# Interleaved partitions for shifted copies, deeper load buffers and a DMA server in the list schedule of an attention and gated convolution kernel

## The chip, the cores and the metric

The kernel runs on one core of a Trainium2 chip. The metric is device time in microseconds (us) of one launch; the kernel before takes 236.15 us, the median of three runs (235.55 to 236.35). The profiled execution has a span of 233.1 us from its first to its last instruction; times inside it are counted from its start.

Names used: PE is TensorE (PEld its weight loads), DVE is VectorE, ACT is ScalarE, POOL is GpSimd, SP is SyncE, whose queue issues nearly all DMAs here. PSUM has eight banks of 128 x 512 floats in this program.

## The reference

Four batches, eight heads, 768 positions, head size 64. Attention is causal, and a query sees only the six chunks of 32 keys with the highest upper bound. The result goes, with heads side by side (512 channels), through a gated unit whose gate is a causal depthwise convolution of five taps.

```python
k_chunks = k.reshape(B, H, nc, chunk, D)                 # chunk = 32, nc = 24
k_min, k_max = np.min(k_chunks, axis=3), np.max(k_chunks, axis=3)
ub = np.sum(np.maximum(q[:, :, :, None, :] * k_min[:, :, None, :, :],
                       q[:, :, :, None, :] * k_max[:, :, None, :, :]), axis=-1)
ub = np.where(causal, ub, -1e9)
top_chunks = np.argsort(ub, axis=-1)[..., -6:]
scores = scale * np.matmul(q, k.transpose(0, 1, 3, 2))
scores = np.where(sel & causal_by_position, scores, -1e9) # sel: the key's chunk is among the six
attn = softmax(scores)
x = np.matmul(attn, v)                                   # then [B, S, 512]

for k in range(5):
    gate_pre += conv_w[k][None, None, :] * xp[:, k:k + S, :]   # xp: x with 4 zero rows ahead
gate = 1.0 / (1.0 + np.exp(-gate_pre))
out = (gate * (x @ w_val)) @ w_out
```

## The kernel before

Work goes by pairs of heads: 16 pairs (0 to 15), four to a batch. For each pair q, k and v are loaded, q and k transposed on PE (`ktr`, `qtr`), the chunk bounds formed (`ub`, `top`), the selection transposed (`selT`), scores computed (`sc`), exponentials taken on ACT (`ex`), multiplied with v (`av`), normalised, and transposed into `xT` (`tox`). The convolution of a pair (`cv`) and, once for each batch of four pairs, the value product (`val`), the gating (`gv`) and the output product (`out`) follow.

Every step is an operation of a graph. A list schedule, run when the program is built, puts the operations of each engine and the DMA issues into a fixed order, and gives each PSUM tile its bank; on the chip each engine works through its own order and waits on semaphores. An operation has an engine, the time that it holds it (`occ`), a latency and a key that ranks it:

```python
NBUF = dict(kn=3, qn=3, vn=3, Kh=3, Qh=3, ql=2, rh=2, rl=2, km=2, KB=2, VA=3, mub=2, top=2, NS=2,
            MT=2, on=2, xT=8, XS=3, g=8, gv=8, osb=3, scr=4)
...
    def op(self, name, eng, occ, key, emit, r=(), w=(), war=(), ps=(), lat=None, mode=None, after=()):
...
                    o.end = t + occ - o.occ + o.lat
```

The loads, two DMAs for each tensor and pair, one for each head:

```python
        def load(name, p=p, b_=b_, h0=h0):
            def emit():
                src = getattr(t, name[0])
                for hh in range(2):
                    t.nc.sync.dma_start(out=vv(name, p)[:, :, hh * 64:(hh + 1) * 64],
                                        in_=src[b_, h0 + hh].rearrange("(t p) d -> p t d", p=128))
            return emit
        for x, name in enumerate(("kn", "qn", "vn")):
            G.op(f"{name}{p}", "SP", 1.1, key("load", p, x + (3 if x == 2 else 0)), load(name), w=[(name, p)], lat=3.2)
```

The convolution uses shifted copies of `xT`. The 128 channels of a pair, in four groups of 32, go to DRAM (`scr`, one row for each of 32 channels, the four groups side by side), and come back four times (`XS`): into partitions 0 to 31 and 32 to 63 as they are, into 64 to 95 and 96 to 127 three positions further on. Blocks 0 and 2 meet the high part of the taps in the matmul, blocks 1 and 3 the low part, so one matmul of 128 rows covers taps o and o + 3 in two precisions. `WD` holds the diagonals of taps that fit this order of partitions.

```python
        def xw(p=p):
            t.nc.sync.dma_start(out=t.scr[p % 4].rearrange("c (g n) -> g c n", g=4), in_=t.xT[:, p % 8, :])

        def xs(p=p):
            n = 4 * XW
            for blk in range(4):
                sh = 3 * (blk // 2)
                t.nc.sync.dma_start(out=vv("XS", p)[32 * blk:32 * blk + 32, 0:n - 3], in_=t.scr[p % 4][:, sh:sh + n - 3])
        G.op(f"xw{p}", "SP", 0.55, key("xs", p), xw, r=[("xT", p)], w=[("scr", p)], lat=2.6)
        G.op(f"xs{p}", "SP", 2.2, key("xs", p, 0.1), xs, r=[("scr", p)], w=[("XS", p)], lat=4.6)

        def conv(w, p=p):
            def emit():
                ...
                for o in range(3):
                    for g in range(4):
                        t.nc.tensor.matmul(out=b[32 * g:32 * g + 32, 0:HB], lhsT=t.WD[:, o * 16 + (p % 4) * 4 + g, :],
                                           rhs=x[:, g * XW + w * HB + o:g * XW + w * HB + o + HB], start=(o == 0), stop=(o == 2))
```

The output tiles: a product into PSUM, an eviction by ACT into one of the `osb` buffers, a store.

```python
        def outev(s, b_=b_):
            def emit():
                t.nc.scalar.activation(out=vv("osb", 6 * b_ + s), in_=bank(("out", b_, s)), func=AF.Copy, scale=0.5)
            return emit

        def outdma(s, b_=b_):
            def emit():
                t.nc.sync.dma_start(out=t.out[b_, s * 128:(s + 1) * 128, :], in_=vv("osb", 6 * b_ + s))
            return emit
```

The weights `wval` and `wout` are loaded once from GpSimd's queue, with a cast to 16 bits.

Of the kernel before, what the change touches and what calls it, by code (L numbers as in the profile page):

```python
# [46 lines left out]
for _bi, _segs in enumerate(BANKS):  # L47
    for _col, _jt, _q0, _n in _segs:
        for _i in range(_n // 128):
            WHERE[_jt, _q0 // 128 + _i] = (_bi, _col + 128 * _i)  # L50

NBUF = dict(kn=3, qn=3, vn=3, Kh=3, Qh=3, ql=2, rh=2, rl=2, km=2, KB=2, VA=3, mub=2, top=2, NS=2,
            MT=2, on=2, xT=8, XS=3, g=8, gv=8, osb=3, scr=4)

PERIOD = 9.537
OFF = dict(load=-38.8, ktr=-26.25, qtr=-23.06, kev=-7.55, qev=-7.41, ksm=-26.91, spl=-1.52, vc=6.87,
# [3 lines left out]

class Op:
    __slots__ = ("name", "eng", "occ", "lat", "emit", "key", "deps", "succ", "ps", "n", "ready", "start",
                 "end", "idx", "mode")


class Graph:
# [3 lines left out]
        self.nbuf, self.ops = nbuf, []  # L70
        self.reads, self.writes, self.wars, self.after = {}, {}, [], []

    def op(self, name, eng, occ, key, emit, r=(), w=(), war=(), ps=(), lat=None, mode=None, after=()):
        o = Op()
        o.name, o.eng, o.occ, o.emit, o.key, o.ps = name, eng, occ, emit, key, tuple(ps)
# [12 lines left out]
        return o  # L88
# [21 lines left out]
    def schedule(self, nbank=8):  # L110
# [8 lines left out]
        mode = None  # L119
        ready = {e: [] for e in ENG}  # L120
        for o in ops:
            o.n, o.ready = len(o.deps), 0.0
# [7 lines left out]
        while events:  # L130
            t = heapq.heappop(events)
            while events and events[0] <= t + 1e-9:
                heapq.heappop(events)
            while releases and releases[0][0] <= t + 1e-9:
                rt, b = heapq.heappop(releases)
                freeb.append((rt, b))
            again = True
            while again:
                again = False
                for e in ENG:  # L140
# [32 lines left out]
                    if e == "PE":  # L173
                        if o.mode != mode:
                            occ += MODE_SWITCH
                        mode = o.mode
                    o.end = t + occ - o.occ + o.lat
                    free_at[e] = t + occ
                    for x in o.ps:
                        b = home[x]  # L180
# [24 lines left out]
ENG = ("PE", "ACT", "DVE", "POOL", "SP")  # L205
SEM = dict(PE=0.24, ACT=0.15, DVE=0.13, POOL=0.10, SP=0.0)
MODE_SWITCH = 0.08


def mm(n, cols):  # L210
# [19 lines left out]
def graph(off, period, nbuf):  # L230
    G = Graph(nbuf)
    t = T()

    def key(stage, p, x=0.0):
        return p * period + off[stage] + x

    def bank(x):
        return t.psb[G.home[x]]
# [4 lines left out]
    def vv(name, v):  # L243
        a = t.tiles[name]
        return a[v % nbuf[name]]
# [58 lines left out]


    def w_cw():
        for b in range(4):
            t.nc.sync.dma_start(out=t.cw4[:, b, :], in_=t.conv_w.rearrange("k (c d) -> (k c) d", d=32))
    kd = 0.9 * period
    G.op("cw", "SP", 2.0, kd + off["load"] + 2 * period, w_cw, w=[("cw4",)], lat=4.0)  # L310
# [4 lines left out]
    G.op("wbig", "POOL", 2.4, 2.2 * period, w_big, w=[("wbig",)], lat=14.0)  # L315

    def w_tr():
        t.nc.tensor.transpose(out=bank("cwT")[:, 0:80], in_=t.cw4.rearrange("p b d -> p (b d)"),
                              identity=t.ident[0:80, 0:80])
    G.op("cwT", "PE", 0.12, 1.2 * period, w_tr, r=[("cw4",), ("ident",)], ps=["cwT"])  # L320

    def w_split():
        nc, b = t.nc, bank("cwT")
        nc.vector.memset(t.wsel, 0.0)
        nc.vector.tensor_copy(out=t.whi, in_=b[:, 0:80])
        nc.vector.tensor_tensor(out=t.wlo, in0=b[:, 0:80], in1=t.whi, op=ALU.subtract)
        for blk in range(4):
            ps_ = slice(32 * blk, 32 * blk + 32)
            src = (t.whi, t.wlo)[blk % 2]
            lo, n = (0, 48) if blk < 2 else (48, 32)  # L330
            nc.vector.tensor_copy(out=t.wsel[ps_, 0:n], in_=src[ps_, lo:lo + n])
            nc.vector.tensor_copy(out=t.id4[ps_, :], in_=t.ident[ps_, ps_])
    G.op("wsplit", "DVE", 1.6, 1.2 * period, w_split, r=[("cwT",), ("ident",)], w=[("wsel",)], ps=["cwT"],
         after=[G.ops[-1]])

    def w_diag(j):
# [9 lines left out]
    for p in range(NPAIR):  # L346
# [3 lines left out]
        def load(name, p=p, b_=b_, h0=h0):  # L350
            def emit():
                src = getattr(t, name[0])
                for hh in range(2):
                    t.nc.sync.dma_start(out=vv(name, p)[:, :, hh * 64:(hh + 1) * 64],  # L354
                                        in_=src[b_, h0 + hh].rearrange("(t p) d -> p t d", p=128))
            return emit
        for x, name in enumerate(("kn", "qn", "vn")):
            G.op(f"{name}{p}", "SP", 1.1, key("load", p, x + (3 if x == 2 else 0)), load(name), w=[(name, p)], lat=3.2)


        def tr(name, w, p=p):
# [74 lines left out]
        G.op(f"rlo{p}", "DVE", dve(640), key("spl", p, 0.1), rlo, r=[("Qh", p), ("ql", p)], w=[("rl", p)])  # L436

        def vcast(p=p):
            t.nc.gpsimd.tensor_copy(out=vv("VA", p)[:, :, :, 0:D].rearrange("p h t d -> p t h d"),
                                    in_=vv("vn", p).rearrange("p t (h d) -> p t h d", h=2))  # L440
        G.op(f"vc{p}", "POOL", 1.05, key("vc", p), vcast, r=[("vn", p), ("ones",)], w=[("VA", p)])


# [147 lines left out]
        def xs(p=p):  # L591
            n = 4 * XW
            for blk in range(4):
                sh = 3 * (blk // 2)
                t.nc.sync.dma_start(out=vv("XS", p)[32 * blk:32 * blk + 32, 0:n - 3], in_=t.scr[p % 4][:, sh:sh + n - 3])
        G.op(f"xw{p}", "SP", 0.55, key("xs", p), xw, r=[("xT", p)], w=[("scr", p)], lat=2.6)
        G.op(f"xs{p}", "SP", 2.2, key("xs", p, 0.1), xs, r=[("scr", p)], w=[("XS", p)], lat=4.6)

        def conv(w, p=p):
            def emit():  # L600
# [20 lines left out]
    for b_ in range(B):  # L621
# [89 lines left out]
def kernel(  # L711
# [17 lines left out]
    def tl(name, shape, dt=FP):  # L729
        return cp.tile(shape, dt, tag=name, name=name)  # L730
# [10 lines left out]
    t.cw4 = tl("cw4", [80, 4, 32])  # L741
    t.whi = tl("whi", [128, 80], F16)
    t.wlo = tl("wlo", [128, 80])
    t.wsel = tl("wsel", [128, 48])
# [8 lines left out]
    shapes = dict(kn=([128, NT, 128], FP), qn=([128, NT, 128], FP), vn=([128, NT, 128], FP), Kh=([128, S], F16),  # L753
                  Qh=([128, S], F16), ql=([128, 640], F16), rh=([128, 640], F16), rl=([128, 640], F16),
                  km=([128, 2, NCH], FP), KB=([128, 2, 2, 2 * NCH], F16), VA=([128, 2, NT, D + 1], F16),
                  mub=([128, NIT, 2 * NCH], FP), top=([128, NIT, 2, 8], FP), NS=([128, NIT, 128], F16),
# [36 lines left out]
```

The softmax here doesn't subtract the row's maximum and nothing guards it: scores larger than these inputs give would overflow.

## Time and profile before

| What | Value |
|---|---|
| time, median of three | 236.15 us |
| span of the profiled execution | 233.1 us |
| PE busy | 191.0 us, 82% |
| DVE busy | 148.2 us, 64% |
| ACT busy | 142.7 us, 61% |
| POOL busy | 96.3 us, 41% |
| DMA by the hardware queue | 41.06 MB, 81.5% of 16 engines |
| mean granted PE clock | 0.912 |

Each view is read as follows. The strip cuts the span into 40 equal slices; a digit is the busy share of a slice in tenths, and for PEclk the granted clock in tenths of full speed. A wait names the engine and line that waited, what released it, the total, how often, and the longest. The chain of waits is followed back from the last instruction; its pieces are given in order of time. A stretch line gives busy time of each engine in the stretch, with the number of instructions, then the clock, the DMA share and the rate. A DMA share above one means that more than one packet at a time was open on an engine.

The DMA issues of the page (KB of one, median us from issue to landing):

```profile
XS<-scr SPq DMA_DIRECT2D x64, 193.3 KB, 4.3
kn<-in_k_dram SPq DMA_DIRECT2D x32, 192.0 KB, 6.3
qn<-in_q_dram SPq DMA_DIRECT2D x32, 192.0 KB, 6.4
vn<-in_v_dram SPq DMA_DIRECT2D x32, 192.0 KB, 5.3
out_dram<-osb SPq DMA_DIRECT2D x24, 256.0 KB, 4.7
scr<-xT SPq DMA_DIRECT2D x16, 193.5 KB
```

### The profile page before, as it was taken

What the parts mean: (1) busy time and instruction counts of PE and PEld (TensorE: products, weight loads), DVE (VectorE), ACT (ScalarE), POOL (GpSimd) and SP (SyncE); (2) the same over time, 40 slices, a digit from 0 to 9 for tenths busy, and PEclk for the clock granted to TensorE, in tenths of its full rate; (3) what the DMA queues carried; (4) which work ended last, traced back from release to release, by engine and by line L of the source; (5) the groups of instructions that cost most, each with busy time, mean ns of one, the idle gap of its engine ahead of it and who ended that gap; (6) DMA issues with size and microseconds to landing.
All of it is one profiled execution on the core that took longest, in us unless ns stands there. A gap on an engine that the chain in (4) does not pass through costs nothing.

```text
span 233.1 us, 7133 instructions
## 1 busy us (share of the span) xinstructions
PE 191.0 (82%) x2713; PEld 129.4 (56%) x2713; DVE 148.2 (64%) x481; ACT 142.7 (61%) x313; POOL 96.3 (41%) x216
## 2 busy tenths in 40 slices
PE   7476599999999994999991059999999999941993
PEld 3364396778666754484750028668475675511441
DVE  2687679999999994688590006998955355300340
ACT  2342849998998893777760055997766982301233
POOL 8766926576874771635260002746422130000000
PEclk9769779999999999799999558999999999995599
DMA  7999999989998999699999999596377845468133
GB/s 158 218 218 140 221 221 209 211 200 187 219 170 200 193 201 185 145 197 178 194 182 196 240 225 212 156 211 167 97 198 192 241 98 145 123 180 257 46 132 138
DMA packets 85377, 42.55 MB, mean 183 GB/s; under 512 B 77152, under 2 KB 80224, under 8 KB 85344
## 3 DMA queue, kind: packets, MB, share of 16 engines
q1 hardware_dynamic: 84288, 41.06, 81.5%
q0 software_dynamic: 1056, 1.05, 2.8%
q8 instruction: 21, 0.34, 0.7%
q14 instruction: 12, 0.10, 0.2%
HBM read 33.68 MB, written 9.46 MB: 185 GB/s over the span
## 4 chain that ended last, share of the span: by engine, by line
PE 45%; DVE 18%; DMA 18%; SPq 10%; issue 4%; ACT 3%; DVEq 0%; ACTq 0%
PE b L628 9%; SPq L354 7%; PE b L605 7%; PE b L652 7%; DMA scr<-xT 5%; DMA qn<-in_q_dram 5%; PE b L365 5%; PE b L554 5%; DMA kn<-in_k_dram 4%; DVE km L377 4%; PE b L510 4%; DVE on L563 4%; PE b L451 3%; PE b L515 3%; DVE ql L415 2%
## 5 line engine op out<-in xcount | busy, mean ns | idle before, releaser
L524 ACT ACTIVATE P<-b 128x512 f16<-128x512 f32 (+1 forms) x192 | 88.3, 584 | 13.6 <-PE b L515 9.6
L532 POOL TENSOR_SCALAR_AFFINE_SELECT P<-P 128x512 f16<-128x512 f16 (+1 forms) x64 | 35.2, 570 | 53.5 <-ACT P L524 52.8
L510 PE MATMUL b<-Qh,Kh 64*128 64x128 f16 (+3 forms) x384 | 40.5, 269 | 13.3 <-ACT osb L658 13.2
L515 PE MATMUL b<-MT,E 64*128 64x128 f16 (+4 forms) x352 | 38.4, 266 | 1.3 <-DVE MT L496 1.3
L377 DVE TENSOR_REDUCE km<-b 128x12 f32<-128x384 f32 x64 | 33.0, 547 | 9.0 <-POOL P L532 3.8
L636 DVE SCALAR_TENSOR_TENSOR gv<-g,b 128x384 f16<-128x384 f32 x32 | 17.5, 549 | 32.0 <-PE b L628 31.4
L658 ACT ACTIVATE osb<-b 128x512 f32<-128x512 f32 x24 | 14.4, 621 | 35.2 <-DMA out_dram<-osb 25.0
L605 PE MATMUL b<-XS,WD 128*32 128x384 f16 x384 | 22.1, 358 | 7.9 <-DMA XS<-scr 7.9
L515 PEld LDWEIGHTS <-E 64*128 64x128 f16 x352 | 18.0, 98 | 18.5 <-issue 15.7
L554 PEld LDWEIGHTS <-P 128*128 128x128 f16 x672 | 24.4, 99 | 4.9 <-issue 2.5
L554 PE MATMUL b<-VA,P 128*128 128x65 f16 x672 | 26.7, 196 | 0.5 <-DVE on L563 0.3
L371 ACT ACTIVATE Kh<-b 128x384 f16<-128x384 f32 x32 | 16.1, 512 | 17.0 <-PE b L365 10.1
L510 PEld LDWEIGHTS <-Kh 64*128 64x128 f16 x384 | 18.8, 97 | 12.4 <-issue 7.9
L628 PE MATMUL b<-xT,wval 128*128 128x384 f16 x128 | 25.6, 344 | 0.0
L652 PE MATMUL b<-wout,gv 128*128 128x512 f16 x96 | 22.2, 380 | 0.1
L407 ACT ACTIVATE Qh<-b 128x384 f16<-128x384 f32 x32 | 14.7, 499 | 11.4 <-PE b L365 11.3
L611 ACT ACTIVATE g<-b 128x384 f32<-128x384 f32 x32 | 15.5, 512 | 9.2 <-PE b L605 4.4
L584 DVE COPY xT<-b 128x768 f16<-128x768 f16 x16 | 8.8, 549 | 19.0 <-PE b L579 16.6
L365 PE MATMUL b<-ident,kn 128*128 128x128 f32 x96 | 15.0, 294 | 6.7 <-DMA kn<-in_k_dram 5.6
L365 PE MATMUL b<-ident,qn 128*128 128x128 f32 x96 | 15.0, 291 | 4.7 <-DMA qn<-in_q_dram 4.7
L563 DVE TENSOR_TENSOR on<-b,rcp 128x384 f16<-128x384 f32 x32 | 17.8, 557 | 1.1
L605 PEld LDWEIGHTS <-WD 128*32 128x32 f16 x384 | 8.9, 101 | 17.1 <-DMA XS<-scr 8.7
(62 smaller groups left out, 322.7 us busy)
## 6 DMA issues: line engine op xcount, KB each, us to landing
XS<-scr SPq DMA_DIRECT2D x64, 193.3 KB, 4.3
kn<-in_k_dram SPq DMA_DIRECT2D x32, 192.0 KB, 6.3
qn<-in_q_dram SPq DMA_DIRECT2D x32, 192.0 KB, 6.4
vn<-in_v_dram SPq DMA_DIRECT2D x32, 192.0 KB, 5.3
out_dram<-osb SPq DMA_DIRECT2D x24, 256.0 KB, 4.7
scr<-xT SPq DMA_DIRECT2D x16, 193.5 KB
wval<-in_moe_w_val_dram POOLq DMA_DIRECT2D x1, 512.0 KB, 7.0
wout<-in_moe_w_out_dram POOLq DMA_DIRECT2D x1, 512.0 KB, 9.9
```

What stands on the lines that cost most here:

```text
L365: t.nc.tensor.transpose(out=b[:, j * 128:(j + 1) * 128], in_=vv(name, p)[:, 3 * w + j, :], identity=t.ident)
L377: t.nc.vector.tensor_reduce(out=vv("km", p)[:, i, w * 12:(w + 1) * 12], in_=bank(("kn", p, w))[:, 0:HB].rearrange("p (c t) -> p c t", t=CH ...
L510: nc.tensor.matmul(out=bb[hh][:, col:col + n], lhsT=kh[HP[hh], jt * 128:(jt + 1) * 128], rhs=qh[HP[hh], q0:q0 + n], start=(si == 0), stop= ...
L515: nc.tensor.matmul(out=bb[hh][:, col + m0 - q0:col + n], lhsT=t.E[HP[hh], jt * 128:(jt + 1) * 128], rhs=mt[HP[hh], m0 - 128:q0 + n - 128], ...
L524: t.nc.scalar.activation(out=t.P[p % 2][hh][bi], in_=bank(("s", p, bi, hh))[:, 0:n], func=AF.Exp, scale=0.125 / QS)
L532: t.nc.gpsimd.affine_select(out=ap, in_=ap, pattern=[[0, n], [1, 128]], compare_op=ALU.is_ge, fill=0.0, base=0, channel_multiplier=-1)
L554: t.nc.tensor.matmul(out=b[:, qt, :], lhsT=t.P[p % 2][hh][bi][:, col:col + 128], rhs=vv("VA", p)[:, hh, jt, :], start=(jt == 0), stop=(jt ...
L563: t.nc.vector.tensor_tensor(out=vv("on", p)[:, :, hh * 64:(hh + 1) * 64], in0=b[:, :, 0:D], in1=rc.unsqueeze(2).to_broadcast([128, NT, D]) ...
L605: t.nc.tensor.matmul(out=b[32 * g:32 * g + 32, 0:HB], lhsT=t.WD[:, o * 16 + (p % 4) * 4 + g, :], rhs=x[:, g * XW + w * HB + o:g * XW + w * ...
L628: t.nc.tensor.matmul(out=k[:, 0:HB], lhsT=t.wval[:, ct, et * 128:(et + 1) * 128], rhs=t.xT[:, (4 * b_ + ct) % 8, 4 + w * HB:4 + (w + 1) * HB],
L636: t.nc.vector.scalar_tensor_tensor(out=vv("gv", 4 * b_ + et)[:, sl], in0=vv("g", 4 * b_ + et)[:, sl], scalar=1.0, in1=bank(("val", b_, et, ...
L652: t.nc.tensor.matmul(out=k, lhsT=vv("gv", 4 * b_ + et)[:, s * 128:(s + 1) * 128], rhs=t.wout[:, et, :], start=(et == 0), stop=(et == NCT - 1))
```

## The change

The four shifted copies are laid out with a partition step of 4: channel d of copy b goes to partition 4d + b, where it was 32b + d. The filter's taps, their high and low parts and the diagonal blocks are prepared for that order (masks made from the identity choose, by partition modulo 4, high or low part and taps o or o + 3). v of a pair comes in one DMA, in an order that the cast to 16 bits reads straight through; the filter comes in one DMA and is replicated by DVE. There are five buffers for q, k and v and four for the output. The list schedule treats DMA as a server that takes one transfer after another, so that it no longer counts on a fixed latency for each; the order of all engines follows from that.

```diff
-NBUF = dict(kn=3, qn=3, vn=3, Kh=3, Qh=3, ql=2, rh=2, rl=2, km=2, KB=2, VA=3, mub=2, top=2, NS=2,
-            MT=2, on=2, xT=8, XS=3, g=8, gv=8, osb=3, scr=4)
+NBUF = dict(kn=5, qn=5, vn=5, Kh=3, Qh=3, ql=2, rh=2, rl=2, km=2, KB=2, VA=3, mub=2, top=2, NS=2,
+            MT=2, on=2, xT=8, XS=3, g=8, gv=8, osb=4, scr=4)
@@ the schedule @@
                     o.end = t + occ - o.occ + o.lat
+                    if o.dma:
+                        dma_free = max(dma_free, t + DMA_HEAD) + o.dma
+                        o.end = max(t + occ, dma_free) + DMA_TAIL
+DMA_HEAD, DMA_TAIL = 1.0, 1.3
@@ the filter @@
-        for b in range(4):
-            t.nc.sync.dma_start(out=t.cw4[:, b, :], in_=t.conv_w.rearrange("k (c d) -> (k c) d", d=32))
+        t.nc.sync.dma_start(out=t.cw, in_=t.conv_w.rearrange("k (c d) -> (k c) d", d=32))
+    def w_rep():
+        t.nc.vector.tensor_copy(out=t.cw4, in_=t.cw.unsqueeze(2).to_broadcast([80, 32, 4]))
-        nc.vector.memset(t.wsel, 0.0)
-        nc.vector.tensor_copy(out=t.whi, in_=b[:, 0:80])
-        nc.vector.tensor_tensor(out=t.wlo, in0=b[:, 0:80], in1=t.whi, op=ALU.subtract)
-        for blk in range(4):
-            ...                       # two copies of 32 partitions for each block
+        v.tensor_reduce(out=t.pm[:, 0:4], in_=t.ident.rearrange("p (c b) -> p b c", b=4), axis=AX.X, op=ALU.add)
+        v.tensor_reduce(out=t.id4, in_=c4, axis=AX.X, op=ALU.add)
+        ...                           # nine more operations on up to 80 columns
@@ the loads @@
+                dst, src = vv(name, p), src[b_, h0:h0 + 2]
+                if name == "vn":
+                    t.nc.sync.dma_start(out=dst, in_=src.rearrange("h (t p) d -> p h t d", p=128))
+                    return
-            G.op(f"{name}{p}", "SP", 1.1, key("load", p, x + (3 if x == 2 else 0)), load(name), w=[(name, p)], lat=3.2)
+            G.op(f"{name}{p}", "SP", 0.6 if x == 2 else 1.1, key("load", p, x + (3 if x == 2 else 0)), load(name), w=[(name, p)], dma=1.8)
@@ the cast of v @@
-            t.nc.gpsimd.tensor_copy(out=vv("VA", p)[:, :, :, 0:D].rearrange("p h t d -> p t h d"),
-                                    in_=vv("vn", p).rearrange("p t (h d) -> p t h d", h=2))
+            t.nc.gpsimd.tensor_copy(out=vv("VA", p)[:, :, :, 0:D], in_=vv("vn", p))
@@ the shifted copies @@
-                t.nc.sync.dma_start(out=vv("XS", p)[32 * blk:32 * blk + 32, 0:n - 3], in_=t.scr[p % 4][:, sh:sh + n - 3])
-        G.op(f"xw{p}", "SP", 0.55, key("xs", p), xw, r=[("xT", p)], w=[("scr", p)], lat=2.6)
-        G.op(f"xs{p}", "SP", 2.2, key("xs", p, 0.1), xs, r=[("scr", p)], w=[("XS", p)], lat=4.6)
+                t.nc.sync.dma_start(out=vv("XS", p)[blk::4, 0:n - 3], in_=t.scr[p % 4][:, sh:sh + n - 3])
+        G.op(f"xw{p}", "SP", 0.55, key("xs", p), xw, r=[("xT", p)], w=[("scr", p)], dma=0.5)
+        G.op(f"xs{p}", "SP", 2.2, key("xs", p, 0.1), xs, r=[("scr", p)], w=[("XS", p)], dma=2.0)
@@ the output stores @@
-            G.op(f"od{b_}.{s}", "SP", 0.6, key("ev", p3, x), outdma(s), r=[("osb", 6 * b_ + s)], lat=2.2)
+            G.op(f"od{b_}.{s}", "SP", 0.6, key("ev", p3, x), outdma(s), r=[("osb", 6 * b_ + s)], dma=0.65)
```

More of the change, by code (lines that the diff above doesn't have):

```diff
@@ L62 @@
     __slots__ = ("name", "eng", "occ", "lat", "emit", "key", "deps", "succ", "ps", "n", "ready", "start",
-                 "end", "idx", "mode")
+                 "end", "idx", "mode", "dma")
 class Graph:
@@ L71, in __init__, with op @@
         self.reads, self.writes, self.wars, self.after = {}, {}, [], []
-    def op(self, name, eng, occ, key, emit, r=(), w=(), war=(), ps=(), lat=None, mode=None, after=()):
+    def op(self, name, eng, occ, key, emit, r=(), w=(), war=(), ps=(), lat=None, mode=None, after=(), dma=None):
         o = Op()
+        o.dma = dma
         o.name, o.eng, o.occ, o.emit, o.key, o.ps = name, eng, occ, emit, key, tuple(ps)
@@ L118, in schedule @@
         free_at = {e: 0.0 for e in ENG}
-        mode = None
+        mode, dma_free = None, 0.0
         ready = {e: [] for e in ENG}
@@ L306, in w_cw @@
     def w_cw():
-        for b in range(4):
-            t.nc.sync.dma_start(out=t.cw4[:, b, :], in_=t.conv_w.rearrange("k (c d) -> (k c) d", d=32))
+        t.nc.sync.dma_start(out=t.cw, in_=t.conv_w.rearrange("k (c d) -> (k c) d", d=32))
     kd = 0.9 * period
-    G.op("cw", "SP", 2.0, kd + off["load"] + 2 * period, w_cw, w=[("cw4",)], lat=4.0)
+    G.op("cw", "SP", 0.6, kd + off["load"] + 2 * period, w_cw, w=[("cw",)], lat=3.0)
     def w_big():
@@ L315, in graph @@
     G.op("wbig", "POOL", 2.4, 2.2 * period, w_big, w=[("wbig",)], lat=14.0)
+    def w_rep():
+        t.nc.vector.tensor_copy(out=t.cw4, in_=t.cw.unsqueeze(2).to_broadcast([80, 32, 4]))
+    G.op("cwrep", "DVE", 0.25, 1.2 * period, w_rep, r=[("cw",)], w=[("cw4",)])
     def w_tr():
-        t.nc.tensor.transpose(out=bank("cwT")[:, 0:80], in_=t.cw4.rearrange("p b d -> p (b d)"),
+        t.nc.tensor.transpose(out=bank("cwT")[:, 0:80], in_=t.cw4.rearrange("p d b -> p (d b)"),
                               identity=t.ident[0:80, 0:80])
@@ L323, in w_split @@
         nc, b = t.nc, bank("cwT")
-        nc.vector.memset(t.wsel, 0.0)
-        nc.vector.tensor_copy(out=t.whi, in_=b[:, 0:80])
-        nc.vector.tensor_tensor(out=t.wlo, in0=b[:, 0:80], in1=t.whi, op=ALU.subtract)
-        for blk in range(4):
[L328 to L333, printed above, removed]
+        v, c4 = nc.vector, t.ident.rearrange("p (c b) -> p c b", b=4)
+        v.tensor_reduce(out=t.pm[:, 0:4], in_=t.ident.rearrange("p (c b) -> p b c", b=4), axis=AX.X, op=ALU.add)
+        v.tensor_reduce(out=t.id4, in_=c4, axis=AX.X, op=ALU.add)
+        v.tensor_tensor(out=t.pm[:, 4:6], in0=t.pm[:, 0:2], in1=t.pm[:, 2:4], op=ALU.add)
+        v.tensor_tensor(out=t.pm[:, 6:7], in0=t.pm[:, 0:1], in1=t.pm[:, 1:2], op=ALU.add)
+        v.tensor_tensor(out=t.pm[:, 7:8], in0=t.pm[:, 2:3], in1=t.pm[:, 3:4], op=ALU.add)
+        v.tensor_copy(out=t.whi, in_=b[:, 0:80])
+        v.tensor_tensor(out=t.wlo, in0=b[:, 0:80], in1=t.whi, op=ALU.subtract)
+        v.tensor_scalar(out=t.wlo, in0=t.wlo, scalar1=t.pm[:, 5:6], scalar2=None, op0=ALU.mult)
+        v.scalar_tensor_tensor(out=t.wlo, in0=t.whi, scalar=t.pm[:, 4:5], in1=t.wlo, op0=ALU.mult, op1=ALU.add)
+        v.tensor_scalar(out=t.wsel, in0=t.wlo[:, 0:48], scalar1=t.pm[:, 6:7], scalar2=None, op0=ALU.mult)
+        v.scalar_tensor_tensor(out=t.wsel[:, 0:32], in0=t.wlo[:, 48:80], scalar=t.pm[:, 7:8], in1=t.wsel[:, 0:32],
+                               op0=ALU.mult, op1=ALU.add)
+    G.op("wsplit", "DVE", 2.0, 1.2 * period, w_split, r=[("cwT",), ("ident",)], w=[("wsel",)], ps=["cwT"],
          after=[G.ops[-1]])
@@ L352, in emit @@
                 src = getattr(t, name[0])
+                dst, src = vv(name, p), src[b_, h0:h0 + 2]
+                if name == "vn":
+                    t.nc.sync.dma_start(out=dst, in_=src.rearrange("h (t p) d -> p h t d", p=128))
+                    return
                 for hh in range(2):
-                    t.nc.sync.dma_start(out=vv(name, p)[:, :, hh * 64:(hh + 1) * 64],
-                                        in_=src[b_, h0 + hh].rearrange("(t p) d -> p t d", p=128))
+                    t.nc.sync.dma_start(out=dst[:, :, hh * 64:(hh + 1) * 64],
+                                        in_=src[hh].rearrange("(t p) d -> p t d", p=128))
             return emit
         for x, name in enumerate(("kn", "qn", "vn")):
-            G.op(f"{name}{p}", "SP", 1.1, key("load", p, x + (3 if x == 2 else 0)), load(name), w=[(name, p)], lat=3.2)
+            G.op(f"{name}{p}", "SP", 0.6 if x == 2 else 1.1, key("load", p, x + (3 if x == 2 else 0)), load(name), w=[(name, p)], dma=1.8)
         def tr(name, w, p=p):
@@ L740 @@
     t.E = tl("E", [128, S], F16)
-    t.cw4 = tl("cw4", [80, 4, 32])
+    t.cw = tl("cw", [80, 32])
+    t.cw4 = tl("cw4", [80, 32, 4])
+    t.pm = tl("pm", [128, 8])
     t.whi = tl("whi", [128, 80], F16)
@@ L752 @@
     t.P = [[[tl(f"P{i}_{hh}{bi}", [128, WIDTH[bi]], F16) for bi in range(6)] for hh in range(2)] for i in range(2)]
-    shapes = dict(kn=([128, NT, 128], FP), qn=([128, NT, 128], FP), vn=([128, NT, 128], FP), Kh=([128, S], F16),
+    shapes = dict(kn=([128, NT, 128], FP), qn=([128, NT, 128], FP), vn=([128, 2, NT, D], FP), Kh=([128, S], F16),
                   Qh=([128, S], F16), ql=([128, 640], F16), rh=([128, 640], F16), rl=([128, 640], F16),
```

## The prediction

> **What bounds the kernel now.** I read the strip of 40 slices first, then the wait list, the queue's own waits, the chain of waits around the two large holes, and last the busy time per stretch. The strip (slices of 5.8 us):
>
> ```profile
> PE   7476599999999994999991059999999999941993
> ...
> PEclk9769779999999999799999558999999999995599
> DMA  7999999989998999699999999596377845468133
> ```
>
> TensorE (PE) is full in most slices and is the bound there. It has three holes: the first six slices, slices 21 to 23 (about 122 to 137 us), and slices 35 to 37 (about 204 to 216 us). The DMA row is full up to slice 24, so transfers are the second bound of the first 140 us. After each of the two later holes the granted clock is 5, half speed. The waits name who holds the middle hole:
>
> ```profile
> engine line waited for: us in total, times, longest us
> ...
> ACT osb L658 <- DMA out_dram<-osb: 25.0, 4, 13.8
> ...
> PE b L510 <- ACT osb L658: 13.2, 1, 13.2
> ```
>
> The score matmul L510 waits 13.2 us in one piece for ScalarE's eviction `osb`, which waits 13.8 us because the tile that was in this buffer before, three output tiles earlier, hasn't gone out. The waits of the queue itself:
>
> ```profile
> SPq L595 <- DMA scr<-xT: 45.1, 12, 5.6
> ```
>
> SyncE's queue is in order. The load of the shifted copies (XS, L595) stands right behind the store of its source (scr) in 12 of 16 cases, and everything behind it, loads and output stores, waits too: 45.1 us. The chain shows how this ends in the holes (start, length, what):
>
> ```profile
> 116.35 5.66 DMA scr<-xT
> 125.49 2.54 SPq L354
> 129.23 0.69 SPq L354
> 130.01 2.12 SPq L663
> 132.22 4.37 DMA out_dram<-osb
> 136.70 0.61 ACT osb L658
> ...
> 202.57 5.99 DMA scr<-xT
> 209.92 4.55 DMA XS<-scr
> 214.52 2.11 PE b L605 x16
> ```
>
> The first output store is issued only at 130.0 us and lands at 136.6. In the tail the last pair goes store, load, convolution with nothing beside it.
>
> Busy time by stretch (time, PE, PEld, DVE, ACT, POOL, clock, DMA share, GB/s):
>
> ```profile
> 2.00:18.00 16.00, 10.79 (x63) 7.64 (x62) 10.17 (x32) 4.74 (x12) 12.42 (x28) 0.79 1.31 221
> 18.00:20.00 2.00, 1.22 (x25) 1.09 (x24) 0.54 (x3) 0.78 (x2) 1.89 (x3) 1.00 0.49 81
> 42.00:90.00 48.00, 45.67 (x817) 34.45 (x811) 45.99 (x158) 44.10 (x100) 32.72 (x72) 1.00 0.99 195
> 90.00:93.00 3.00, 0.28 (x3) 0.31 (x4) 1.13 (x3) 0.02 (x1) 0.00 (x0) 1.00 1.11 195
> 120.00:137.00 17.00, 3.84 (x32) 1.84 (x30) 2.40 (x14) 3.04 (x7) 1.71 (x2) 0.74 0.95 210
> ```
>
> From 42 to 90 us PE is at 95% and VectorE (DVE) at 96%: a faster DMA brings nothing there. At 90 us PE waits 2.8 us for a q load. And the tail by single microseconds:
>
> ```profile
> 211.00:212.00 1.00, 0.00 (x0) 0.00 (x0) 0.00 (x0) 0.00 (x0) 0.00 (x0) 0.50 1.21 217
> 212.00:213.00 1.00, 0.00 (x0) 0.00 (x0) 0.00 (x0) 0.00 (x0) 0.00 (x0) 0.50 0.80 192
> 213.00:214.00 1.00, 0.00 (x0) 0.00 (x0) 0.00 (x0) 0.00 (x0) 0.00 (x0) 0.50 0.96 336
> 214.00:215.00 1.00, 0.48 (x8) 0.29 (x12) 0.00 (x0) 0.00 (x0) 0.00 (x0) 0.50 0.97 373
> ```
>
> Up to 213 us the XS copies are moving, at about 217 GB/s with the engines fully busy; behind them the output stores, which span 128 partitions, run at 336 to 373.
>
> [...] the q, k and v loads have runs of 64 floats, 256 B, and the trace shows 217 to 221 GB/s with only loads moving (2 to 18 us). Nothing in the change lengthens these runs. [...] 0.50 from 211 us on, after idleness since 207.6.
>
> **The change, part by part.**
> 1. XS with partition step 4. A set is four DMAs of 193.3 KB = 792,000 bytes: 3.65 us at 217 GB/s, an estimated 2.1 us at 373 GB/s. 1.5 us x 16 = 24 us of DMA time saved, of which only what falls into DMA-limited places counts.
> 2. v in one DMA: the same 256 B runs, so the same 393,216 bytes / 217 GB/s = 1.81 us. It saves an issue. In the built program every DMA waits for the one eight places before it, so eight in flight now hold more bytes. The filter load goes from four DMAs (2.24 us of queue, 15.5 to 17.8 us) to one; the dip to 81 GB/s at 18 to 20 us should shrink, worth up to 1.2 us of loads. The longer DVE preparation (eleven instructions and the replication in place of eleven small ones of 0.1 to 0.24 us) costs about 0.5 us once. I count +0.5 us for the head in all.
> 3. Five load buffers, four output buffers, and the new order. In the order of the built program the loads run further ahead (those of pairs 0 to 8 stand ahead of the first scr store; before, those up to q of pair 6), ten loads and stores stand between the first scr store and its XS load, where there were two, and convolution 0 moves from after score 4 to after score 6. From pair 11 on the PE order is as before.
>
> Middle hole. If it vanished, PE would win 13.2 us, the clock loss after it (24 convolution matmuls 2.11 against 1.17 us, 37 value matmuls 2.05 against about 1.3: 1.7 us), the 2.8 us at 90 us and the slow clock behind that, about 1.5 us: 19.2 us. But does the store come in time? What DMA must move before the first output store: before, 44 loads x 1.81 + 6.5 (both weight matrices: the software queue's 2.8% of 233) + 8 scr x 0.53 + 7 XS x 3.65 = 116 us, and it was issued at 130, so 14 us were lost to the in-order waits. After, all 48 loads stand ahead of it: 86.9 + 6.5 + 7 x 0.53 + 6 x 2.1 = 110 us. With 3 to 5% lost it lands at 113 to 118 us. PE needs it at output matmul 0.4: score 1 began at 33.4 us, eight pairs of 8.3 us (score 8 began at 94.1, so (94.1 - 33.4 - 2.8) / 7), eight val groups of 0.66 us and four output groups of 0.9 us give about 109. So I expect a wait of some 5 us here, with 0.7 us of clock: the middle brings 19.2 - 5.7 = 13.5 us.
>
> Tail. XS 14 and XS 15 each move 1.5 to 2 us sooner, so the last hole of 6.9 us falls to about 3.2, and the 0.96 us before it goes: 4.5 us, plus perhaps half of the clock loss (convolution 0.94, val 1.9): 1.4 us. Tail: 6.
>
> Sum: 13.5 + 6 + 0.5 = 20 us: 236.15 - 20 = 216.
>
> **The rivals.** (A) DMA keeps up fully and PE is the only bound: 19.2 + 6 + 0.5 = 25.7, so 210.5 us. For it: PE is at 90% or more in most slices anyway. Against it: 110 us of transfers before a store needed at 109. (B) DMA stays the bound: the source reads from HBM, [...] set XS's pace, so XS stays near 3.6 us, the order is all that helps, the store lands near 125 us; the middle brings about 4 and the tail 1: 231 us. For it: XS rate was seen only at one place, with one partition pattern. Against it: [...] stores to HBM in the same place reach 373. (C) The new order costs: val groups 0.00 to 0.20 now come before the convolution whose gate they wait for, so up to four of eight PSUM banks are held over one or two pairs, and scores wait for banks; some 5 us, 221. (D) The weights are issued one value cast earlier, among the first loads, and delay pair 2; they move the same bytes before kn3, so at most 1 to 2 us.
>
> **Range and chances.** 216 lies between A (210.5) and C (221). The range of 208 to 227 holds A, C and half of B. For slower than 241 every gain would have to fail and the new order cost 5 us more: 0.04. Within 2% (231.4 to 240.9) is B with a cost: 0.08. Faster: 0.88.
>
> **What would show it.** The XS landing time falls from 4.3 us, and with XS alone moving GB/s passes 300 (step 1); if it stays at 217, B is right. The queue's wait for scr falls from 45.1 us to the part after pair 7. PE's single wait of 13.2 us becomes one of about 5 at output 0.4 (zero: A). In the tail the wait before the last convolution falls from 6.9 to about 3. Waits of scores on ScalarE or DVE between 65 and 90 us would show C. The prediction is wrong if the middle hole stays at 10 us or more, or if a new wait of such size appears.

## The result

The changed kernel takes 230.2 us (median of four runs, 228.65 to 230.37) against 235.94 us for the kernel before beside it: a ratio of 0.9745 on record (0.976 from these two medians), 95% interval 0.9705 to 0.9785. The span of the profiled execution falls from 233.1 to 226.9 us, by 6.2, where 20 were predicted. For three of the experiments below (the filter first, the DMA server off, and step and rows on the kernel before) the profiled execution was a disturbed one, over 1.5% slower than the fastest of its kernel, so of those only the ratios are used unless the text says so.

The strip of the changed kernel (slices of 5.7 us, counted from 1):

```profile
PE   7273687899999977979999489999999999960993
...
PEclk9766569999999996999999969999999999996799
DMA  8999999999779789996798837435455734278033
```

The middle hole of PE, three slices before, is one slice (the 23rd) with a 4. In its place there are shallow losses from slice 15 on. The first six slices are emptier than before and their clock is lower (5 and 6 in slices 5 and 6). The hole of the tail is still there (slices 36 and 37).

The wait list, reader first, then what released it:

```profile
ACT osb L673 <- DMA out_dram<-osb: 10.2, 3, 4.9
...
PE b L620 <- DMA XS<-scr: 9.5, 3, 6.6
...
DVE cw L322 <- DMA cw<-in_moe_conv_w_dram: 6.1, 1, 6.1
```

ScalarE's wait for the output stores fell from 25.0 to 10.2 us and no longer takes PE down in one piece. Convolutions wait 9.5 us for their copies (7.9 before), and DVE stands 6.1 us for the filter, which is new. The queue's own wait for the scratch store, and the landing of the copies:

```profile
SPq L610 <- DMA scr<-xT: 36.2, 9, 5.4
```

```profile
XS<-scr SPq DMA_DIRECT2D x64, 193.3 KB, 3.0
```

The copies land in 3.0 us instead of 4.3. The store in front of them is as slow as it was: 36.2 us in nine waits is 4.0 each, the longest 5.4 (45.1 in twelve before, 3.8 each). The chain of waits at the start, in the middle and at the end (start, length, what):

```profile
13.55 10.73 DMA vn<-in_v_dram
24.34 0.84 POOL VA L455
...
127.11 2.95 DMA out_dram<-osb
130.17 0.60 ACT osb L673
...
199.01 4.97 DMA scr<-xT
204.04 0.47 SPq L610
204.56 0.59 SPq L610
205.20 0.58 SPq L610
205.83 3.44 DMA XS<-scr
209.40 2.11 PE b L620 x23
```

In the tail the scratch store holds 5.0 us (6.0 before), then come four issues of up to 0.59 us, then the landing of the last copy. The issues themselves got longer: the median is 0.59 us for a copy with the partition step, 0.41 before.

Where both kernels begin the same matmul groups (us from the start of the span, by the trace; the last column is after minus before):

| first matmul of | before | after | difference |
|---|---|---|---|
| score, pair 1 | 33.45 | 37.48 | +4.0 |
| score, pair 5 | 64.92 | 69.05 | +4.1 |
| score, pair 11 | 145.71 | 141.34 | -4.4 |
| score, pair 15 | 184.95 | 180.31 | -4.6 |
| convolution 15 | 214.52 | 209.40 | -5.1 |
| last output | 228.16 | 222.08 | -6.1 |

The head lost 4.0 us, the middle won 8.7, the tail 1.5. Between pairs 5 and 11 the two orders differ, so single groups there are not comparable.

### The profile page after: what moved, and what is told of

Its sections match the earlier page's. It is cut to its first block, busy times and chain, and to the rows that moved or that the text cites. A ratio compares the mean times of both kernels' runs of the same rounds, so it can differ in the third digit from the quotient of the medians.

```text
span 226.9 us, 7101 instructions
## 1 busy us (share of the span) xinstructions
PE 191.1 (84%) x2713; PEld 129.1 (57%) x2713; DVE 147.3 (65%) x482; ACT 142.9 (63%) x313; POOL 97.1 (43%) x216
## 4 chain that ended last, share of the span: by engine, by line
PE 47%; DVE 15%; DMA 14%; SPq 11%; POOL 5%; ACT 4%; issue 3%; ACTq 0%; POOLq 0%; DVEq 0%
PE b L667 7%; PE b L643 7%; PE b L525 7%; PE b L569 6%; PE b L620 5%; PE b L530 5%; SPq L610 5%; DVE km L393 5%; DMA vn<-in_v_dram 5%; SPq L370 5%; DMA scr<-xT 5%; PE b L466 4%; PE b L381 3%; DMA XS<-scr 3%; ACT P L539 2%
## 5 line engine op out<-in xcount | busy, mean ns | idle before, releaser
L525 PE MATMUL b<-Qh,Kh 64*128 64x128 f16 (+3 forms) x384 | 42.0, 271 | 0.7 <-ACT P L539 0.4
L530 PE MATMUL b<-MT,E 64*128 64x128 f16 (+4 forms) x352 | 39.0, 268 | 0.7 <-DVE MT L511 0.7
L620 PE MATMUL b<-XS,WD 128*32 128x384 f16 x384 | 21.3, 350 | 11.6 <-DMA XS<-scr 9.5
L673 ACT ACTIVATE osb<-b 128x512 f32<-128x512 f32 x24 | 14.1, 631 | 19.9 <-DMA out_dram<-osb 10.2
L643 PE MATMUL b<-xT,wval 128*128 128x384 f16 x128 | 25.1, 335 | 0.1
L423 ACT ACTIVATE Qh<-b 128x384 f16<-128x384 f32 x32 | 15.0, 499 | 10.4 <-PE b L381 9.9
L466 PE MATMUL b<-KB,rh 128*128 128x96 f16 x80 | 15.4, 213 | 7.3 <-POOL KB L418 5.7
L455 POOL CAST VA<-vn 128x768 f16<-128x768 f32 x16 | 15.8, 985 | 6.5 <-DMA vn<-in_v_dram 5.2
```

Source lines behind the costliest of these rows:

```text
L466: t.nc.tensor.matmul(out=b[:, i * 96:(i + 1) * 96], lhsT=lhsT, rhs=kb[:, m].rearrange("p a c -> p (a c)"), start=(k == 0), stop=(k == 3))
L525: nc.tensor.matmul(out=bb[hh][:, col:col + n], lhsT=kh[HP[hh], jt * 128:(jt + 1) * 128], rhs=qh[HP[hh], q0:q0 + n], start=(si == 0), stop= ...
L530: nc.tensor.matmul(out=bb[hh][:, col + m0 - q0:col + n], lhsT=t.E[HP[hh], jt * 128:(jt + 1) * 128], rhs=mt[HP[hh], m0 - 128:q0 + n - 128], ...
L643: t.nc.tensor.matmul(out=k[:, 0:HB], lhsT=t.wval[:, ct, et * 128:(et + 1) * 128], rhs=t.xT[:, (4 * b_ + ct) % 8, 4 + w * HB:4 + (w + 1) * HB],
```

## The experiments

Ratios are to the kernel before, run beside each on the same chip; the changed kernel's is 0.9745. "Its order kept" means that the list schedule's order is taken as it is and only the named operations are moved.

**The head: filter or weights.** Two kernels that each move one thing.

```diff
 G, t, order, nbuf = plan()
+move(['cw'], 'kn0')          # cw_first: the filter DMA ahead of all loads
+move(['wbig'], 'vc2')        # w_back: the weight DMAs behind the value cast of pair 1
```

> Start of the kernel. The changed kernel with its order kept, but the filter DMA issued before all loads. The changed kernel's span is 226.9 us; score 1 begins at 37.5 us there and at 33.5 us in the kernel before. Theory F (the late filter and DVE's in-order wait of 6.1 us for it cost the head): the wait of 6.1 us is gone, score 1 begins at about 33.5 us, the span falls by about 4 us to 223. Theory W (the weight matrices, issued at 11.3 us in place of 17.3 us, hold up the q of pair 2 and all behind it): the DVE wait is gone but PE still waits for q of pair 2 until about 22.5 us, score 1 begins at 36 us or later, the span falls by 1 us at most.

> Start of the kernel. The changed kernel with its order kept, but the two weight DMAs moved back to where the kernel before has them in GpSimd's order, behind the value cast of pair 1. Theory W: q of pair 2 is transposed at about 17.5 to 19 us instead of 22.9, the filter lands at about 19 to 20 us, score 1 begins at about 33.5 us and the span falls by about 4 us to 223. Theory F: the filter's landing still sits behind the loads of pair 2, DVE still waits for 3 us or more, score 1 begins at 36 us or later, and the span falls by less than 2 us.

With the filter first: ratio 0.980 (0.973 to 0.987). With the weights back: ratio 0.981 (0.975 to 0.986), span 227.7 us. Neither is faster than the changed kernel. But the weights are the cause of the slow head: with them back, q of pair 2 is transposed at 19.9 us instead of 22.9 and score 1 begins at 31.8 us instead of 37.5, 1.7 us earlier than in the kernel before. Theory W is right about the head and wrong about the end. At score 5 the lead over the changed kernel is still 5.7 us (63.3 against 69.05); at score 7 it is 0.6 (96.7 against 97.2). The wait list of this kernel shows where it went:

```profile
PE b L620 <- DMA XS<-scr: 15.7, 4, 6.9
```

PE waits 15.7 us for the copies, 6.2 more than in the changed kernel. PE got there earlier and the copies did not. On this reading DMA sets the pace up to there, and the head is worth nothing until DMA is faster; the runs with the rows below put that to the test.

**The step, with the new order kept.** Copies back on 32 adjacent partitions, the filter prepared for that order.

```diff
-out=vv("XS", p)[blk::4, 0:n - 3]
+out=vv("XS", p)[32 * blk:32 * blk + 32, 0:n - 3]
```

> The changed kernel with its order, buffers and v loads kept, but the four shifted copies back on 32 adjacent partitions each (and the filter prepared for it). Theory S (step 4 doubles the rate of the copies and that is what the change lives from): median landing of XS goes from 3.0 back to 4.3 us, six sets ahead of the first output store cost 1.5 us more each, the two waits of ScalarE for an output store (3.4 and 1.9 us) grow to some 12 us together, span 234 to 238, slower than the kernel before. Rival O (order and buffers brought the gain, the rate of the copies little): span within 2 us of 226.9.

Ratio 1.037 (1.030 to 1.044), span 242.9 us: worse than the kernel before.

```profile
PE b L616 <- DMA XS<-scr: 20.5, 5, 6.5
...
ACT osb L669 <- DMA out_dram<-osb: 14.5, 3, 5.6
```

```profile
XS<-scr SPq DMA_DIRECT2D x64, 193.3 KB, 3.9
```

Theory S holds, and more strongly than expected (span 234 to 238), although the copies land in 3.9 us and not in 4.3, and a packet of a copy takes 236 ns in the changed kernel against 421 in the kernel before, which is 1.8 times the rate and not double: under this order, which was made for fast copies, the step is worth 6% (1.037 / 0.9745 = 1.064). Without it, the new order and buffers make the kernel slower than before.

**The DMA server off.** All parts of the change, but the list schedule counts on the fixed latencies of before.

```diff
-w=[(name, p)], dma=1.8)
+w=[(name, p)], lat=3.2)
```

(and likewise `lat=2.6`, `4.6` and `2.2` for the scratch, the copies and the output)

> The changed kernel with every part of the change except the DMA server: the list schedule counts on the old fixed latencies again and makes its own order, in which the convolutions stand early again and the weights behind the value cast of pair 1. Theory C (the new order costs: value groups hold PSUM banks and pairs 6 to 8 run slower, weights too early): the head is back at 33.5 us for score 1, scores 7 and 8 come no later than 84 and 95 us, span 217 to 222. Rival Q (without the new order the load of the copies stands right behind its store again and blocks loads and output stores): the queue's wait for scr is above 45 us, the middle hole is 8 us or more, span 226 to 232.

Ratio 1.016 (1.009 to 1.023), 1.6% slower than before. Rival Q has the direction right and the size too small: its span of 226 to 232 would still have been a gain. Five load buffers and one v load with an order made for fixed latencies lose 4% against the server's order (1.016 / 0.9745 = 1.043). Theory C, that the new order is what costs, expected 217 to 222 and misses by far; but this run puts the old kind of waits in the place of the new order's costs, so it does not measure those.

**The scratch store.** The stretches of half a microsecond after a store's issue at 154.73 us in the changed kernel, when little else moves (time, PE, PEld, DVE, ACT, POOL, clock, DMA share, GB/s):

```profile
156.00:156.50 0.50, 0.50 (x15) 0.50 (x13) 0.50 (x2) 0.19 (x1) 0.48 (x2) 1.00 0.26 87
156.50:157.00 0.50, 0.50 (x10) 0.37 (x7) 0.50 (x2) 0.34 (x1) 0.00 (x0) 1.00 0.30 90
157.00:157.50 0.50, 0.50 (x8) 0.37 (x7) 0.50 (x3) 0.15 (x1) 0.00 (x0) 1.00 0.31 79
157.50:158.00 0.50, 0.50 (x9) 0.50 (x7) 0.50 (x3) 0.00 (x0) 0.00 (x0) 1.00 0.24 50
158.00:158.50 0.50, 0.50 (x6) 0.39 (x5) 0.50 (x3) 0.43 (x2) 0.32 (x2) 1.00 0.27 96
158.50:159.00 0.50, 0.50 (x5) 0.29 (x3) 0.50 (x2) 0.45 (x2) 0.41 (x2) 1.00 0.23 87
```

A share of 0.23 to 0.31 is about 4 of 16 engines, and the rate stays under 100 GB/s for three microseconds. The trace's record of single packets agrees: of the 128 packets of this store (1548 bytes each) four are open at once for half of the time, and never more than six; which engines they were on, the record does not say. The store's access pattern in memory has four outer rows (the channel groups) of 32 x 774. That the four rows are what keeps four packets open is a conjecture here. The test gives the store 128 outer rows: the scratch has 128 rows, and the store stays one DMA. The layout of the scratch changes with it, and the copies are read back in four runs.

```diff
-scr = dr.tile([32, 4 * XW], F16)
+scr = dr.tile([128, XW], F16)
-out=t.scr[p % 4].rearrange("c (g n) -> g c n", g=4), in_=t.xT[:, p % 8, :]
+out=t.scr[p % 4], in_=t.xT[:, p % 8, :]
-out=vv("XS", p)[blk::4, 0:n - 3], in_=t.scr[p % 4][:, sh:sh + n - 3]
+out=vv("XS", p)[blk::4, 0:n].rearrange("c (g n) -> c g n", g=4)[:, :, 0:XW - 3],
+in_=t.scr[p % 4].rearrange("(g c) n -> c g n", g=4)[:, :, sh:sh + XW - 3]
```

> The changed kernel, its order kept, with the scratch laid out as 128 rows so that the store of the pair goes out with 128 outer rows instead of 4 groups (one DMA as before), and the copies read back in four runs of 1542 bytes. With the old layout the store alone moved 81 to 96 GB/s at a DMA share near 0.3 (142 to 144 us in the changed kernel), as if on four of the sixteen engines. Theory K (the store on few engines is the transfer that sets the pace of the first 130 us and of the tail): the wait from store to copies falls from about 5 us to 3 or less, the first output store is issued at 112 to 116 us instead of 122, the last hole falls from 6.6 to about 4 us, span 212 to 218. Rival N (the 256-byte loads alone set the pace; the store is latency): the store still needs 4.5 us or more, span within 2 us of 226.9. Rival P (four times as many packets in the copies cost as much as the store saves): landing of XS rises above 3.6 us, span 226 or more.

Ratio 0.920 (0.910 to 0.930), median 216.3 us, span 214.7 us: inside theory K's range. The same kind of stretch, after a store's issue at 151.98 us in this kernel:

```profile
152.00:152.50 0.50, 0.50 (x8) 0.43 (x7) 0.50 (x2) 0.01 (x1) 0.00 (x0) 1.00 0.20 49
152.50:153.00 0.50, 0.50 (x8) 0.50 (x6) 0.50 (x2) 0.07 (x1) 0.04 (x1) 1.00 0.30 115
153.00:153.50 0.50, 0.50 (x6) 0.34 (x4) 0.50 (x2) 0.50 (x2) 0.42 (x2) 1.00 0.72 260
153.50:154.00 0.50, 0.50 (x5) 0.29 (x3) 0.50 (x3) 0.31 (x1) 0.38 (x2) 1.00 0.06 9
```

The same bytes are through in 1.5 us, with a share of 0.72 at the peak; up to 17 of its packets are open at once, against six. The strip, and the last convolution in the timeline (start, length, what, and in brackets the idle time before it):

```profile
PE   7384378799999998978999969999999999996992
...
PEclk9958558999999999999999999999999999999999
```

```profile
198.99 1.17 PE L621 MATMUL b<-XS,WD 128*32 128x384 f16 x24 [2.17 <-DMA XS<-scr]
```

```profile
SPq L610 <- DMA scr<-xT: 16.6, 7, 3.6
```

The first output store is issued at 116.1 us instead of 122.3. Of the middle hole a slice with a 6 is left (the 24th), in which ScalarE waits 3.7 us once for an output store. The last hole is 2.2 us instead of 6.6, and the clock stays up after the head, so the 24 convolution matmuls take 1.17 us and not 2.11. The queue waits 16.6 us for the store instead of 36.2; from store issue to first copy issue the tail still takes 3.5 us, where theory K had 3 or less. Score 11 begins 5.1 us earlier than in the changed kernel and the last output 12.2 us earlier: 5 from the middle and 7 from the tail. The copies land in 3.5 us with their shorter runs (3.0 before): rival P is real but small. The head is as slow as in the changed kernel, score 1 at 38.4 us.

**Rows or engines?** The run above changed the layout of the scratch as well. This one leaves layout and copies alone and from pair 8 on splits the store into four DMAs of 32 outer rows.

```diff
+for g in range(4):           # for pairs 8 to 15; one DMA as before for 0 to 7
+    t.nc.sync.dma_start(out=dst[g], in_=t.xT[32 * g:32 * g + 32, p % 8, :])
```

> The changed kernel with the scratch laid out as it was, the copies read in 6186-byte runs as they were, but from pair 8 on the store is issued as four DMAs, each of 32 outer rows. Theory K (it is the number of outer rows, 4, that keeps the store on few engines): from pair 9 on store to copies takes 3.5 to 4 us although three more issues stand in between, the last hole falls from 6.6 us to about 4, the clock stays up, span 218 to 222. Rival L (it was the other layout in memory or the shorter runs that helped): store to copies stays at 5 us or more and the span at 226 or more.

Ratio 0.944 (0.936 to 0.953), span 223.5 us. The queue in the tail (start, length with all four issues, line):

```profile
189.65 2.96 SPq L609 DMA_DIRECT2D scr<-xT  x4
193.97 2.37 SPq L615 DMA_DIRECT2D XS<-scr  x4
196.39 1.98 SPq L609 DMA_DIRECT2D scr<-xT  x4
...
200.03 2.37 SPq L615 DMA_DIRECT2D XS<-scr  x4
```

From first store issue to first copy issue it takes 3.6 and 4.3 us with three issues more in between; in the changed kernel the tail took 5.0. With the store split, up to 16 of its packets are open at once, against six with one DMA. The last hole is 3.5 us, against the 4 of theory K. The clock, which theory K expected to stay up, fell to half at 207.1 us. The span is 1.5 us above the range given, as the tail gained only 3.4 us, about half of the 7 that the rows won there. Rival L falls as the whole account: that part of the gain needs neither the layout nor the run length. This run has four DMAs where there was one, but the run with the rows has one; so the number of DMAs is not what both have in common, and the number of outer rows is.

**The store alone, on the kernel before.** The rows of the scratch, in the kernel before and nothing else.

> The kernel before with nothing but the scratch as 128 rows. Theory K: the queue's wait for scr falls from 45 us to about 25, the middle hole shrinks by 5 us or more and the tail hole by 2, span 220 to 227 against 233.1. Rival N: within 2 us of 233.1.

Ratio 0.9475 (0.936 to 0.959), span 221.5 us. Two changed access patterns, without any reordering, are worth twice what the whole change under study is.

```profile
PE b L510 <- ACT osb L659: 10.9, 1, 10.9
```

```profile
SPq L595 <- DMA scr<-xT: 28.7, 12, 5.0
```

The span is in theory K's range, and the last hole falls by 2.8 us to 4.1. The wait for scr falls from 45.1 to 28.7 us (about 25 expected), and the middle hole only from 13.2 to 10.9, where 5 us or more were expected: the store's rate is the lesser part of it.

**The step alone, on the kernel before.**

> The kernel before with nothing but the partition step of 4 (and the filter prepared for it); its order, buffers and loads are kept. If the step alone brings what it brings under the new order (the changed kernel is 6% faster with it than without): span 218 to 224. If it needs the new order, because under the old one the waits in the queue and not the rate of the copies decide: landing of XS falls to about 3 us all the same, the queue's wait for scr stays near 45 us, span 228 to 233.

Ratio 0.9745 (0.962 to 0.987), span 228.8 us.

```profile
ACT osb L663 <- DMA out_dram<-osb: 27.0, 4, 17.1
...
PE b L515 <- ACT osb L663: 16.4, 1, 16.4
```

```profile
SPq L600 <- DMA scr<-xT: 46.0, 12, 4.9
```

The span is in the range of the second expectation, and so is the mechanism: the copies land in 2.9 us, the waits for scr stay at 46.0 us, and the middle hole even grows from 13.2 to 16.4. The gain lies ahead of it and behind it: score 11 begins 1.7 us earlier than in the kernel before (144.0 against 145.7), the last output 4.3 us earlier (223.9 against 228.2). The point estimate is that of the whole change.

**Step and rows, on the kernel before.**

> The kernel before, its order, buffers and loads kept, with the partition step of 4 and the scratch as 128 rows. So far, as ratios to the kernel before: step alone 0.9745, rows alone 0.9475, all parts of the change 0.9745, all parts and rows 0.920. If order, buffers and the single load of v are worth nothing once DMA is fast enough: ratio 0.91 to 0.93, span 213 to 217. If they are what keeps the output stores from waiting: the middle hole stays at 7 us or more, ratio 0.935 to 0.95, span 218 to 221.

Ratio 0.917 (0.912 to 0.922), against 0.920 (0.910 to 0.930) with order, buffers and the single v load as well. In sum those three parts are worth nothing that these runs can tell. That is a balance and not an absence of effects: with the rows, the old order keeps its middle hole (10.9 us in the run above; 10.0 in the disturbed profile of this one, over the 7 of the second expectation), while the new order clears it but for the 3.7 us above and loses some 5 us in the head. Where the new order gives up the rest of what it wins is not known.

**The weights again, with the rows.**

> The same with the weight DMAs moved back behind the value cast of pair 1. With the old scratch this regained 5.7 us at score 1 and nothing at the end, as the copies' loads made PE wait anyway. Theory K: with the pace of DMA raised, the head's gain is kept, 3 to 5 us less than the run with the scratch rows alone. Rival: DMA's pace still decides, less than 1 us.

Ratio 0.911 (0.899 to 0.923), span 212.4 us, 2.3 less than with the rows alone. Score 1 begins 5.9 us earlier and 2.3 are left at the end: between the two expectations, and the intervals of the ratios overlap, so it is a likely gain and not a shown one. At the last convolution it is still 3.7 us earlier; the rest is the clock. The hole before that convolution is 2.6 us here, and the clock falls to half in it, so that the 24 matmuls take 2.11 us; with the rows alone the hole is 2.2 us and the clock stays up.

**The last loads behind the output stores.**

```diff
+move(['kn15', 'qn15', 'vn15'], 'xs7')
```

> The changed kernel, its order kept, but the loads of pair 15 moved behind the output stores 0.0 to 0.3 in the queue. Theory V (the output stores behind the last loads hold up output 0.4): the two waits of ScalarE for an output store, 3.4 and 1.9 us, vanish, span 221 to 223. Rival (DMA is behind as a whole, so what moves ahead is paid by what moves back, or by the copies of pairs 5 to 7): span within 1.5 us of 226.9.

Ratio 0.961 (0.949 to 0.973), span 223.2 us, 3.7 less than the changed kernel. ScalarE's waits of 3.4 and 1.9 us in the middle are gone, as theory V has it. So by the profile the stores' place in the queue cost some of what was missing; by the ratio this is not shown, as the interval overlaps that of the changed kernel (0.9705 to 0.9785).

**All together.** The changed kernel with the rows, the filter first, the weights behind the loads of pair 3 and the last loads behind output stores.

> The changed kernel, its order kept but for three moves, with the scratch as 128 rows, the filter DMA first, the weights behind the loads of pair 3 (before the value cast of pair 3), and the loads of pair 15 behind four output stores. If each of the three adds to what the 128 rows brought: span 208 to 211. If the pairs 5 to 9 are now bound by PE and by banks held for the value groups, so that the head's gain is lost there as before: 212 to 214.7.

Ratio 0.901 (0.894 to 0.909), span 213.8 us. The second expectation holds: the three moves add little to the rows. This has the lowest ratio of all. Its interval ends at 0.909 and that of the rows alone begins at 0.910; but the kernel before ran slower beside this run (median 238.5 us against 236.1), and the medians are 214.2 and 216.3 us, so a small gain over the rows is likely and no more. From the rows with the weights back (0.899 to 0.923) it is not told apart.

## Why the prediction was wrong

1. **Copies with partition step 4: the mechanism right, the saving too large.** In the tail of the changed kernel the copies move at about 300 GB/s:

```profile
206.00:207.00 1.00, 0.00 (x0) 0.00 (x0) 0.00 (x0) 0.67 (x2) 0.00 (x0) 0.70 1.04 316
207.00:208.00 1.00, 0.00 (x0) 0.00 (x0) 0.00 (x0) 0.00 (x0) 0.00 (x0) 0.50 0.91 287
```

against 217 and 192 in the lines of the prediction (one microsecond ahead of those, the copies of before had 260). A packet of a copy (6186 bytes) took 421 ns before and takes 236 ns now, the median of 2048 in each trace, with the source read in the same way. So rival B, in which reading held the copies back, is refuted. That the step would bring the copies to the 373 GB/s of the output stores, and so a set to 2.1 us, was the author's estimate: no trace of before has a copy with it. A set does not shrink from 3.65 to 2.1 us. Its four issues of 0.59 us alone need about 2.4, and by the packets the sets of pairs 8 to 15 take 3.1 to 3.8 us from first to last, against 4.0 to 5.3 before: some 0.8 us less, not 1.5.

2. **The middle, -13.5 us: the step that failed, by its size.** At score 11 the changed kernel is 4.4 us ahead, where the prediction had 14 (13.5 and the head's 0.5). The mechanism, that DMA work ahead of the first output store decides how far the scores get, fits: in the four versions of the changed kernel in this table, score 11 begins 19.0 to 20.1 us after that store is issued. It is not all: with the last loads behind the output stores the first of these is issued 8.8 us earlier (113.5), and score 11 begins only 3.4 us earlier.

| us from the start of the span | first output store issued | score 11 | last output |
|---|---|---|---|
| kernel before | 130.0 | 145.7 | 228.2 |
| kernel before, rows | 124.6 | 139.0 | 216.5 |
| changed kernel | 122.3 | 141.3 | 222.1 |
| changed, weights back | 122.6 | 141.8 | 222.8 |
| changed, rows | 116.1 | 136.2 | 209.9 |
| changed, rows, weights back | 113.0 | 132.1 | 207.6 |

The term "7 x 0.53" for the scratch stores was wrong. It took 373 GB/s, the rate of the output stores in the tail. Alone the store moves at 50 to 96 GB/s, so its 198,000 bytes need 2.1 us at the best of these rates. As an estimate, seven stores then need 7 x (2.1 - 0.53) = 11 us more, which turns 110 into 121 us, and the store was issued at 122.3. That this comes so close is in part luck. Measured, the rows bring the store forward by 6.2 us under the new order, and by 9.5 with the weights back in both kernels (122.6 to 113.0). Then it stands some 3% over the sum of 110, where the prediction allowed for 3 to 5%. The kernel before has the same term (116 us against an issue at 130, the 14 us put down to in-order waits): there the rows bring 5.4 us. That the rest comes from the in-order waits, as the prediction had it, is possible and not shown.

The prediction's own sign of being wrong, a middle hole of 10 us or more, did not come. The one wait of 13.2 us is gone; in its place PE has pieces of 1.7 to 2.1 us between 84 and 131 us. With 128 rows the median is 216.3 us, where the prediction had 216. That agreement is luck too: against the kernel before, that run wins 14.8 us in the middle and 8.5 in the tail, more than the 13.5 and 6 of the prediction, and loses 5.0 in the head.

3. **The tail, -6 us: the saving for a set and the store.** The prediction gave each of the last two sets 1.5 to 2 us and left the store between them out of its sum. The four issues of the last set in the kernel before (start, length, line):

```profile
208.62 1.72 SPq L595 DMA_DIRECT2D XS<-scr  x4
```

From the first of them to the landing of the last copy at 214.47 it took 5.85 us, and 5.23 in the changed kernel (204.04 to 209.27): 0.6 us less. The last landing is 1.1 us shorter, and the longer issues take back half of that. The store still took 5.0 us of the last chain (6.0 before). Store issue to last convolution went from 214.52 - 202.57 = 11.95 to 209.40 - 199.01 = 10.4 us. With the rows it is 198.99 - 189.58 = 9.4, and the last store is issued 9.4 us earlier where score 15 begins 5.1 us earlier, so it has less of a backlog ahead of it; the hole is 2.2 us and the clock doesn't fall. The clock is worth 1.8 us of the tail there (convolution 1.17 against 2.11 us, the 24 value matmuls behind it 4.01 against 4.87). The prediction read the clock as 0.50 from 211 us on, after idleness since 207.6; the stretch from 210 to 211 has 0.54 already, so it fell after some 2.5 us, and with the rows and the weights back it fell in a hole of 2.6 us.

4. **The head, +0.5 us: wrong in sign.** It lost 4.0 us at score 1. Rival D, early weights, had been priced at 1 to 2 us because the bytes ahead of k of pair 3 are the same. But it is q of pair 2 and the filter that need their place: q of pair 2 was transposed 5.5 us later (22.9 against 17.4 us), and DVE, which works in order, stood 6.1 us for the filter. Putting the weights back recovers 5.7 us there. With the old store it did not cost the end much, since DMA's pace took it away by score 7; with the rows, putting the weights back brings the first output store forward by 3.1 us.

5. **Rivals.** A (210.5) needs the rows and the head: the rows with the weights back have a median of 214.6 us. C was not measured by itself: the run with the DMA server off mixes it with waits in the queue. Its own sign, scores waiting on ScalarE or DVE between 65 and 90 us, is absent: there the score matmuls wait for nothing, and 0.7 us in the whole kernel. With step and rows the old order and the new one end together, so what the new order costs is about what it gains. That the parts of order and buffers gain nothing in sum was not among the rivals.

What stays open: which part of the new order costs what it gains. And the run with the DMA server off shows that the buffers and the single v load are no help under the old latencies, but not which of them hurts.

## What to carry to other kernels

A transfer's bytes and its rate in a busy stretch are not enough for a sum. Look at each kind of transfer where it runs alone, and read the DMA share with the rate: here a steady share of 0.23 to 0.31 at 50 to 96 GB/s went with four outer rows in the access pattern, and with 128 rows the same bytes were through in 1.5 us instead of three. Count the issues of a transfer, too, before its bytes: four of 0.59 us were longer than the 2.1 us that the bytes of a set were to take. When a gain at one end of a kernel is gone some stages later, look for the in-order queue or engine that both versions reach at the same time, and mend that first.

## What the runs showed of the hardware

- One store of 198,000 bytes with four outer rows held a DMA share of 0.23 to 0.31 for three microseconds, with four packets open at once for half of the time and never more than six, and one with 128 rows was through in 1.5. On the kernel before, the 128 rows alone brought the ratio to 0.9475.
- With the partition step of 4, a 6186-byte packet of a copy takes 236 ns instead of 421 on 32 adjacent partitions (medians of the two kernels).
- The partition step makes each issue longer: a copy DMA takes 0.59 us of the queue with it and 0.41 without.
- The partition step of the copies alone turned the same order of work from 3.7% slower than the kernel before to 2.6% faster.
